# Attention features and a Fourier mixer on one core: rows in blocks of 32, heads in pairs, and a new order of the work

## The chip, the core and the metric

The kernel runs on one core of a Trainium2 chip. A core has TensorE (PE in the profile; its weight loads are PEld), VectorE (DVE), ScalarE (ACT), GpSimd (POOL) and SyncE (SP, which here only issues DMAs). The engines run side by side, each works through its own instructions in order, and semaphores make one wait for another. DMAs are issued by SP, ACT and POOL and run on 16 DMA engines that all three share; those from POOL are queue q0 in the profile, those from SP queue q1. The metric is the time of one execution on the device in microseconds (us), the median of several runs.

## The reference

Inputs: q, k, v of 8 batches x 8 heads x 576 rows x 64, float32; a projection w_phi 64 x 128; two weights of a feed-forward layer, 512 x 2048 and 2048 x 512.

```python
def phi(x):
    proj = np.einsum('bhsd,df->bhsf', x, w_phi)
    proj = proj - np.max(np.abs(proj), axis=-1, keepdims=True)
    return np.concatenate([np.exp(proj), np.exp(-proj)], axis=-1)
q_p, k_p = phi(q), phi(k)
kv = np.einsum('bhsf,bhsd->bhfd', k_p, v);  z = np.sum(k_p, axis=2)
attn = np.einsum('bhsf,bhfd->bhsd', q_p, kv) / (np.einsum('bhsf,bhf->bhs', q_p, z)[..., None] + 1e-06)

x = attn.transpose(0, 2, 1, 3).reshape(B, S, H * D)            # 8 x 576 x 512
u = x + np.real(np.fft.fft(np.fft.fft(x, axis=1), axis=2))
un = (u - mean(u)) / np.sqrt(var(u) + 1e-06)                    # over the last axis
out = u + np.maximum(un @ w_ch1, 0.0) @ w_ch2
```

## The kernel before

One batch (576 rows) is the unit of work, and eight batches follow one another in a pipeline. For each batch k and q are turned so that their 64 features lie on the partitions (KT, QT), multiplied by w_phi on TensorE, and the row maxima of the absolute value are taken by DVE (MK, MQ). ACT forms both exponentials (KPp, KPn, QPHP, QPHN). The factor that the maximum puts on a row is moved elsewhere: for k it multiplies v (VCp, VCn, V4P, V4N, done by POOL), for q it is the ratio E2 of the negative half to the positive half, which DVE multiplies in when the two halves of a head are combined (`tg`, `cb`), before the division (`rd`, and X by POOL). The Fourier transform along the rows uses its symmetry: row r and row 576 - r are folded together (R, CEO), so rows are stored in an order in which a row and its mirror stand on the same partition. The row transform gives DT and ET (from psums `psD` and `px`, with `pm` for the mean row), the column transform gives `pu`, which is added to X. The normalised rows UN are turned to UT (by TensorE in batch 0, by DMA transposes in the others), the first feed-forward product gives `psf` and HT, the second `pso`, and the result is stored.

The 576 rows stand in five chunks of up to 128: chunks 0 and 1 hold rows 1 to 256 (even and odd), chunk 4 holds the 64 rows 0 and 257 to 319, and chunks 2 and 3 hold rows 320 to 575. Before, rows stand in blocks of 16 within the chunks, turned round block by block; q is loaded as it comes (QS01, QS23), the projection reads it through a pattern with a negative step, and the maxima, which stand in load order, are put in order by two matmuls with a 0/1 matrix TURN (`weigh_q`, psum `pt`). TURN itself is built by DVE from counted numbers.

Batch 0 has code of its own. Its float32 inputs are loaded by SP into the space of tiles that are used later: k and q into that of W2b (as KF, Q01, Q23), the last 64 rows and v into that of HT (`load_first`); TensorE turns them (`turn_part`, psum `pst`). SP's loads are issued in the order k, its last 64 rows, k, q 1 to 256, q 320 to 575, the last q rows, the last v rows, v. The weights W1b (2 MB in bfloat16) and W2b are loaded and cast by POOL's DMAs (`load_ffn_weights`), as are k, q and v of the later batches (KS, QS, VS). While batch 0 is prepared, TensorE has little to do, and `stir` runs 60 matmuls on a constant.

What runs when is written out by hand. Each part of the work is a generator (`STREAMS`): F is the feed-forward layer of a batch in 68 steps, M the key-value products, combination and Fourier mixing, T the exponentials, P the maxima of q, R those of k, S the scaling of v, N the normalisation, W the load of the weights, Z the memsets of padding, C and H the constants, G and J the first turns, Y the `stir` matmuls, K, V, Q the loads of the later batches. The string `PLAN` has one letter for each step, and the instructions of all engines are issued in this order; an engine never departs from it.

Of the kernel before, what the change touches and what calls it, by code (L numbers as in the profile page):

```python
# [10 lines left out]
ALU = mybir.AluOpType  # L11
# [12 lines left out]
    "CCZCYYZYGGCTZVTRZKGTGRZWGJTTSJYRSJTQTTPPYTYRPTJMRJTMSMMSPSTKPTPTZMYTMMQTMTPMCQTMMTMTBDMHKMHKHDDHYAHY"  # L24
    "DYMYMHYTMMVMRTQMTNMMYTNTQNNYSFNMFNFNRVRFSTTPTFMFRSYUNTFWMURFVFFFFUUMTPMFBSTFMNTUTPNUSMFVPPCTFMFTUPQM"
    "TFMFTFPATVMFFFMMFTFMFKMFFMQFMFRTKFMFFRFPFDFFFFTFFFFTDFFFDRTFFFMFFTTDMFRFFFFSFFMFFFTFMSMFRFTMTTNMTFMN"
    "FPTMMFSSMTPMFTPPMTFFFMFFQNMPTFBSFMFFQMFFPTFFMNNUAMFFMFMFVTRTFFMFFVRVFFKMFKFFFFTMFMFFFFQMFPFDFFTPFRFF"
    "FTFDPFFTFFDDFFRFFTMFFFTMFFMMBSFFMSFRFTMMTFTNNFMFMMMKFTFMTSTFFFFSMPPTMTFFFFFMFSFMFPTMQQVFFFPTKFFMNNNM"
    "FFMFFMFFUMFFMFMFFFAMTRTVFFRTVFFFFFQMFFFDFDFTFFFDRFTPDFFFTPFFRFFTMFFFFTMMMFSFFRSFTMFTFMTTFNFTFMFNSMMM"
    "FMBSFKTTMQNFFFNPFMTFFFMFTPPFMFSFMNFPQMUTFVFKFPAFFMMFMFFVMFFMTFMFFMFFFMRTFRVFFTFFFQMFFFFTDDFRFFFFTFDP"  # L30
    "FFDFTPFFFRFTMTFFFFFMMMFFRFSFSTMSTFFMTFTFFNMFFTNMMMMSTTFMFFQNFTFPMFFFMFVNFMTBPPFSFMFFTPFMKFFFMFFQPNMF"
    "FMAUKFFMFFFMTTFRFRFMFFFTSFFFFVTMFFFRMTQFFFMTFFFFDFDFFFRFDFTFFDMFTFMFFMFSMFMRFTFFTMFTFTFFTMNNFPSMMMMV"
    "TFFSMTPMSTQFFMTPMFTFBQMFPPPFFMFFMFNVFPFFANNUMFFMFMTFMFFMFFMFFRTFRMFFFFFFFVTTPFSFFRFVFFMTFDFFTFFFDFDR"
# [7 lines left out]
def kernel(  # L41
# [39 lines left out]
    magic = const.tile([128, 1], F32, name="magic")  # L81
    nc.vector.memset(magic[:], -MAGIC)
# [25 lines left out]
    TURN = const.tile([128, 2, 128], F32, name="TURN")  # L108
# [39 lines left out]
    def count_first():  # L148
        count(pc_i[:, 0:1], [[1, 1]], 0, 1)
        count(pc[:, 0:2], [[1, 2]], 225, 2)  # L150
        count(pc[:, 2:3], [[1, 1]], 256, 1)
        nc.gpsimd.memset(pc[0:1, 2:3], 0.0)
        for j in range(2):
            count(
                rs[:, 128 * j:128 * j + 128].rearrange("p (a r) -> p a r", r=16),
                [[-32, 8], [2, 16]], 225 + j, 0,
            )
        count(rs[:, 256:NK], [[1, 64]], 256, 0)
        nc.gpsimd.memset(rs[:, 256:257], 0.0)
        count(tn[:, 0, :], [[1, 128]], 0, -1)  # L160
        nc.vector.tensor_single_scalar(
            out=ident[:], in_=tn[:, 0, :], scalar=0.0, op=ALU.is_equal
        )
        count(pc[:, 3:4], [[1, 1]], 128, -1)
        count(rc.rearrange("p (a r) -> p a r", a=2), [[1, 2], [2, 256]], 0, 0)

    def count_rest():
# [8 lines left out]
        count(tn[:, 1, :], [[1, 128]], 0, 1)  # L176
# [5 lines left out]
    def constants(b):  # L182
        nc.vector.tensor_single_scalar(
            out=pc_i[:, 1:2], in_=pc_i[:, 0:1], scalar=4, op=ALU.arith_shift_right
        )
# [5 lines left out]
        nc.vector.tensor_scalar_mul(out=pn[:, 0:3], in0=pc[:, 0:3], scalar1=1.0 / S)
        nc.vector.tensor_scalar_mul(out=pn[:, 3:4], in0=pc[:, 3:4], scalar1=1.0 / C)
        for j in range(3):
# [29 lines left out]
        yield  # L223
        for t, n in enumerate((112.0, 15.0)):
            nc.vector.tensor_scalar(
                out=blk[:, 1 + t:2 + t], in0=pc_i[:, 1:2], scalar1=64.0 * t - 32.0,
                scalar2=n, op0=ALU.mult, op1=ALU.add,
            )
            nc.vector.tensor_scalar(
                out=TURN[:, t, :], in0=tn[:, t, :], scalar1=blk[:, 1 + t:2 + t], scalar2=None,  # L230
                op0=ALU.is_equal,
            )
# [60 lines left out]
    def make_q(b):  # L293
# [4 lines left out]
            (QS[:], q[b, :, at:at + 256, :].rearrange("h (p j) d -> p h (j d)", j=2))  # L298
            for QS, at in ((QS01, 1), (QS23, 320))
# [23 lines left out]
    def load_first():  # L323
# [105 lines left out]
    def features(b):  # L429
# [977 lines left out]
```

## Time and profile before

| | |
|---|---|
| runs | 426.52 us median of 3 (426.04 to 428.52) |
| profiled execution | span 423.1 us from the first to the last instruction; its runs' median is 3.4 us above the span |
| busy, of the span | PE 94%, PEld 61%, DVE 78%, ACT 72%, POOL 49% |
| chain that ended last | PE 61%, DVE 20%, ACT 8%, POOL 5%, DMA 2%, issue 2% |
| TensorE clock granted | 0.999 of full speed |
| DMA | 42.70 MB, mean 101 GB/s |

Rows of groups read: line, engine, operation, output <- inputs, shapes, count | total busy us, mean ns of one | idle time of the engine just ahead. The mean of a matmul is its length in the pipeline; several overlap, so the total divided by the count is the distance from one to the next. Rows of the timeline read: start us, duration us, engine, line, operation, and in square brackets how long the engine was idle before it and what ended that. Rows of stretches give for each engine its busy us and the number of instructions, then the granted clock, the DMA engines' busy share and GB/s. DMA rows give packets, MB and the share of 16 engines' time.

### The profile page before, as it was taken

What the parts mean: (1) busy time and instruction counts of PE and PEld (TensorE: products, weight loads), DVE (VectorE), ACT (ScalarE), POOL (GpSimd) and SP (SyncE); (2) the same over time, 40 slices, a digit from 0 to 9 for tenths busy, and PEclk for the clock granted to TensorE, in tenths of its full rate; (3) what the DMA queues carried; (4) which work ended last, traced back from release to release, by engine and by line L of the source; (5) the groups of instructions that cost most, each with busy time, mean ns of one, the idle gap of its engine ahead of it and who ended that gap; (6) DMA issues with size and microseconds to landing.
All of it is one profiled execution on the core that took longest, in us unless ns stands there. A gap on an engine that the chain in (4) does not pass through costs nothing.

```text
span 423.1 us, 10390 instructions
## 1 busy us (share of the span) xinstructions
PE 397.4 (94%) x4093; PEld 256.1 (61%) x4122; DVE 331.1 (78%) x681; ACT 306.3 (72%) x626; POOL 207.8 (49%) x271
## 2 busy tenths in 40 slices
PE   8787798999899999999999999999999999999995
PEld 3454475744676558655675558665766567656563
DVE  4989788798979976998779885898989786968103
ACT  6978799748975899489847898588868887353460
POOL 7982688525646077706673282834755331500000
PEclk9999999999999999999999999999999999999999
DMA  8999959984569468853899069954895081103313
GB/s 218 206 165 163 148 88 174 145 83 76 89 102 180 72 101 106 123 84 49 112 153 138 2 91 136 131 71 66 117 138 77 14 102 32 27 0 72 72 26 87
DMA packets 108761, 42.70 MB, mean 101 GB/s; under 512 B 82857, under 2 KB 103721, under 8 KB 108713
## 3 DMA queue, kind: packets, MB, share of 16 engines
q0 software_dynamic: 45936, 16.60, 37.1%
q1 hardware_dynamic: 62215, 24.85, 34.8%
q8 instruction: 32, 0.52, 0.5%
q10 hardware_dynamic: 562, 0.59, 0.5%
q14 instruction: 16, 0.13, 0.1%
HBM read 36.77 MB, written 9.44 MB: 109 GB/s over the span
## 4 chain that ended last, share of the span: by engine, by line
PE 61%; DVE 20%; ACT 8%; POOL 5%; DMA 2%; issue 2%; DVEq 0%; ACTq 0%; POOLq 0%
PE psf L1224 21%; PE pso L1241 19%; DVE R L903 3%; PE kv L887 3%; DVE cb L999 3%; DVE tg L994 2%; PE pso L1267 2%; PE psD L1045 2%; DMA UT<-UN 2%; PE pu L1104 2%; PE psq L547 1%; DVE MK L511 1%; PE psk L491 1%; PE psh L597 1%; DVE X L1094 1%
## 5 line engine op out<-in xcount | busy, mean ns | idle before, releaser
L1224 PE MATMUL psf<-UT,W1b 128*128 128x320 bf16 (+1 forms) x1024 | 142.5, 286 | 2.4 <-DMA UT<-UN 1.5
L1241 PE MATMUL pso<-W2b,HT 128*128 128x512 bf16 x467 | 117.1, 379 | 1.7 <-issue 0.5
L1224 PEld LDWEIGHTS <-W1b 128*128 128x128 bf16 x1024 | 94.0, 98 | 29.7 <-issue 4.3
L1229 ACT ACTIVATE HT<-psf 128x320 bf16<-128x320 f32 x128 | 53.5, 442 | 27.0 <-PE psf L1224 21.6
L1241 PEld LDWEIGHTS <-HT 128*128 128x128 bf16 x496 | 44.8, 98 | 44.6 <-issue 2.6
L1002 POOL TENSOR_TENSOR X<-cb,rd 128x320 f32<-128x320 f32 x56 | 41.5, 746 | 38.6 <-DVE rd L1001 37.3
L466 POOL TENSOR_TENSOR VCn<-VS,VCn 128x512 bf16<-128x512 bf16 x28 | 29.7, 1061 | 38.1 <-ACT VCn L461 35.3
L1231 ACT ACTIVATE HT<-psf 128x512 bf16<-128x512 f32 x64 | 37.9, 605 | 12.6 <-PE psf L1224 12.0
L555 DVE TENSOR_REDUCE MQ<-psq 128x8 f32<-128x1024 f32 (+1 forms) x32 | 34.3, 1084 | 13.4 <-PE psq L547 13.2
L1247 DVE SCALAR_TENSOR_TENSOR X<-pso,rs,X 128x512 f32<-128x512 f32 x31 | 22.8, 735 | 21.6 <-PE pso L1241 21.6
L497 ACT ACTIVATE KPn<-psk 128x1024 bf16<-128x1024 f32 x28 | 28.6, 1021 | 14.0 <-DVE MK L511 13.9
L497 ACT ACTIVATE KPp<-psk 128x1024 bf16<-128x1024 f32 x28 | 28.7, 1025 | 11.1 <-PE psk L491 11.1
L451 POOL TENSOR_TENSOR V4N<-VS,V4N 64x256 bf16<-64x256 bf16 x14 | 8.7, 623 | 53.9 <-ACT V4N L447 53.4
L511 DVE TENSOR_REDUCE MK<-psk 128x8 f32<-128x1024 f32 x28 | 33.9, 1212 | 1.0 <-ACT KPp L497 0.7
L1094 DVE TENSOR_TENSOR X<-pu,X 128x512 f32<-128x512 f32 (+3 forms) x49 | 23.3, 526 | 11.2 <-PE pu L1104 8.9
L466 POOL TENSOR_TENSOR VCp<-VS,VCp 128x512 bf16<-128x512 bf16 x28 | 29.7, 1059 | 0.0
L606 ACT ACTIVATE QPHP<-psh 128x1024 bf16<-128x1024 f32 x28 | 28.9, 1031 | 0.8 <-PE psh L597 0.6
L606 ACT ACTIVATE QPHN<-psh 128x1024 bf16<-128x1024 f32 x28 | 29.0, 1035 | 0.0
L1150 ACT ACTIVATE UN<-X,MV 128x512 bf16<-128x512 f32 (+1 forms) x35 | 24.5, 723 | 5.4 <-DVE MV L1175 3.1
L1174 DVE BATCH_NORM_STATS2 st<-X 128x6 f32<-128x512 f32 (+1 forms) x40 | 27.1, 677 | 0.3
L1190 POOL TENSOR_TENSOR rs<-VE,mhalf 128x5 f32<-128x5 f32 (+1 forms) x9 | 10.3, 1145 | 29.0 <-DVE VE L1189 29.0
L987 PEld LDWEIGHTS <-QPHP 128*128 128x128 bf16 x280 | 21.2, 99 | 4.6 <-DVE cb L999 1.0
(465 smaller groups left out, 825.0 us busy)
## 6 DMA issues: line engine op xcount, KB each, us to landing
out_dram<-X SPq DMA_DIRECT2D x15, 256.0 KB
out_dram<-X SPq DMA_DIRECT2D x60, 64.0 KB
QS<-in_q_dram POOLq DMA_DIRECT2D x14, 256.0 KB, 6.2
KS<-in_k_dram POOLq DMA_DIRECT2D x7, 512.0 KB, 7.4
VS<-in_v_dram POOLq DMA_DIRECT2D x14, 256.0 KB, 5.1
W1b<-in_moe_w_ch_dram POOLq DMA_DIRECT2D x1, 2048.0 KB, 13.1
W2b<-in_moe_w_ch_dram POOLq DMA_DIRECT2D x1, 2048.0 KB, 14.8
W2b<-in_k_dram SPq DMA_DIRECT2D x2, 512.0 KB
```

The source lines that it names most:

```text
L466: nc.gpsimd.tensor_tensor(out=VC[:, hs, :, 0:D], in0=values[b][0][:, hs, :].rearrange("p h (j d) -> p h j d", d=D), in1=VC[:, hs, :, D:D + ...
L497: nc.scalar.activation(out=KP[:, hs, :, :].rearrange("p e (jp jj) f -> p jj (e jp) f", jj=2), in_=psk[:], func=AT.Exp, scale=sgn,)
L511: nc.vector.tensor_reduce(out=MK[:, 2 * pr:2 * pr + 2, :].rearrange("p e (jp jj) -> p jj (e jp)", jj=2), in_=tiles[pr][:], axis=AX.X, op=A ...
L555: nc.vector.tensor_reduce(out=o, in_=i[:], axis=AX.X, op=ALU.max, apply_absolute_value=True)
L606: nc.scalar.activation(out=o, in_=psh[:], func=AT.Exp, scale=sgn)
L1002: nc.gpsimd.tensor_tensor(out=X[:, :, D * h:D * h + D], in0=cb[:, :, 0:D], in1=rd[:].to_broadcast([128, 5, D]), op=ALU.mult,)
L1094: nc.vector.tensor_tensor(out=to, in0=more, in1=to, op=ALU.add)
L1174: nc.vector.bn_stats(out=st[0:M, :], in_=X[0:M, c, 0:C])
L1224: nc.tensor.matmul(ps, lhsT=W1b[:, cc, 128 * hh:128 * hh + 128], rhs=UT[:, cc, lo:hi], start=(cc == 0), stop=(cc == NCC - 1),)
L1229: nc.scalar.activation(out=HT[:, hh, lo:hi], in_=ps, func=AT.Relu, scale=-1.0)
L1231: nc.scalar.activation(out=HT[:, hh - 1:hh + 1, lo:hi], in_=psw[:].rearrange("p (a n) -> p a n", a=2), func=AT.Relu, scale=-1.0,)
L1241: nc.tensor.matmul(po[:], lhsT=HT[:, hh, at:at + 128], rhs=W2b[:, hh, :], start=(hh == 0), stop=(hh == NHH - 1),)
```

## The change

- Rows stand in blocks of 32 instead of 16. Chunks 0 and 1 are loaded block by block, already in order (four DMAs of 32 partitions instead of one of 128, in every later batch); chunks 2 and 3 still need the turn within a block, which for the maxima is now one `stream_shuffle` on DVE. TURN, its construction and its matmuls go, and with them some of the constants' steps. Stores of chunks 0 and 1 are four instead of eight a batch.
- The maxima of the last 64 q rows are formed on 128 partitions, two head pairs at once: 4 matmuls for 8, a DVE reduction of half the length, a POOL copy that brings the upper half down and a POOL memset.
- Two neighbouring heads are divided and scaled in one go (one `rd`, one X for two heads), in the order 0, 1, 6, 7, 4, 5, 2, 3.
- The second product of the last 64 rows: before, even and odd hidden blocks went to the two halves of the PSUM partitions, 512 columns each, and were added one after the other; now each hidden block goes to both, 256 columns each.
- Batch 0: k is loaded by head pair (four DMAs for two), w_phi by one DMA; the row transform takes two single banks and splits its copies otherwise; one pass of the constants moves from ACT to DVE.
- `PLAN` is another string.

```diff
-        for e in range(2):
-            nc.scalar.dma_start(out=wphi_f[64 * e:64 * e + 64, :], in_=w_phi[:, :])
+        nc.scalar.dma_start(out=wphi_f[:], in_=w_phi[:, :].unsqueeze(0).to_broadcast([2, D, DF]))
-        for g in range(2):
-            hs = slice(4 * g, 4 * g + 4)
+        for n, pr in enumerate(PAIRS):
+            hs = slice(2 * pr, 2 * pr + 2)
             put(KF[:, hs, :], k[0, hs, 0:512, :].rearrange("h (p j) d -> p h (j d)", j=4))
...
         def qmax4():
+            whole = pj.tile([128, 2, 4, DF], F32, tag="pj", name="psq4")
+            for s in range(2):
                 for e in range(2):
                     rr = slice(64 * e, 64 * e + 64)
                     nc.tensor.matmul(
-                        ps[e][:, pr, :], lhsT=QT4[rr, pr, :], rhs=wphi2[rr, :],
+                        whole[:, e, s, :],
+                        lhsT=QT4[rr, 2 * s:2 * s + 2, :].rearrange("p x n -> p (x n)"),
+                        rhs=wphi2[rr, :], start=True, stop=True,
...
+            nc.vector.tensor_reduce(
+                out=m[:, 0], in_=whole[:, :, 0:2], axis=AX.X, op=ALU.max, apply_absolute_value=True
+            )
+            nc.gpsimd.tensor_copy(out=m[0:64, 1], in_=m[64:128, 0])
+            nc.gpsimd.memset(m[64:128, 0], 0.0)
...
         def weigh_q(hs):
-            pt = pk.tile([128, n, 4], F32, tag="pk", name="pt")
-            for t in range(2):
-                nc.tensor.matmul(
-                    pt[:, :, 2 * t:2 * t + 2], lhsT=TURN[:, t, :],
-                    rhs=mq[:, hs, 2 * t:2 * t + 2], start=True, stop=True,
-                )
-            nc.scalar.activation(
-                out=E2[:, hs, 4:5], in_=mq[:, hs, 4:5], func=AT.Exp, scale=2.0
-            )
-            nc.scalar.activation(out=E2[:, hs, 0:4], in_=pt[:], func=AT.Exp, scale=2.0)
+            nc.vector.stream_shuffle(
+                out=mq[:, hs, 2:4], in_=mq[:, hs, 2:4], mask=list(range(31, -1, -1))
+            )
+            nc.scalar.activation(out=E2[:, hs, :], in_=mq[:, hs, :], func=AT.Exp, scale=2.0)
...
         for hh in range(NHH):
-            g = 64 * (hh % 2)
-            nc.tensor.matmul(
-                po[g:g + 64, :], lhsT=HT[:, hh, 512:576], rhs=W2b[:, hh, :],
-                start=(hh < 2), stop=(hh >= NHH - 2),
-            )
+            for g in range(2):
+                nc.tensor.matmul(
+                    po[64 * g:64 * g + 64, 0:256], lhsT=HT[:, hh, 512:576],
+                    rhs=W2b[:, hh, 256 * g:256 * g + 256], start=(hh == 0), stop=(hh == NHH - 1),
+                )
...
-        for h in (0, 7, 1, 6, 4, 2, 5, 3):
+        for h in (0, 1, 6, 7, 4, 5, 2, 3):
...
 PLAN = (
-    "CCZCYYZYGGCTZVTRZKGTGRZWGJTTSJYRSJTQTTPPYTYRPTJMRJTMSMMSPSTKPTPTZMYTMMQTMTPMCQTMMTMTBDMHKMHKHDDHYAHY"
+    "YYZCGZGZTTCGGRTWCRZCTJYTSJTRTGPSYTJSRYPTTPJTJMMYZRSSMMPKTPTTPMMTKTMMTQQPMMMQVTBTCMTHHDYMMHDAYYHYKYDT"
```

What the new string does to the engines' own orders is seen best on POOL and ACT, in batch 0. POOL before, from the first products of the constants (gs) to the first scaled values (V4N, V4P, VCn, VCp from v in HT's space); W1b is the load of the first weight, VS and KS are loads of batch 1, HI, V4P, V4N, QPHP and QPHN are memsets:

```order
L197 TENSOR_SCALAR gs<-ga,pn 128x320 x3
L268 MEMSET QPHP 128x8x64
L268 MEMSET QPHN 128x8x64
L212 TENSOR_SCALAR gc<-gc,pn 128x512
L215 TENSOR_SCALAR gc<-gc 128x512
L218 TENSOR_TENSOR ga<-ga,gc 128x512
L271 MEMSET V4P 128x520
L284 DMA VS_249<-in_v_dram 64x4x64 x2
L271 MEMSET V4N 128x520
L284 DMA KS_265<-in_k_dram 64x8x64
L274 MEMSET HI_105 128x512
L274 MEMSET HI_106 128x512
L93 DMA W1b<-in_moe_w_ch_dram 128x4x2048
```

And of the change, the same place and on to the first values:

```order
L242 MEMSET QPHP 128x8x64
L181 TENSOR_SCALAR gs<-ga,pn 128x320 x3
L242 MEMSET QPHN 128x8x64
L245 MEMSET V4P 128x520
L91 DMA W1b<-in_moe_w_ch_dram 128x4x2048
L245 MEMSET V4N 128x520
L196 TENSOR_SCALAR gc<-gc,pn 128x512
L199 TENSOR_SCALAR gc<-gc 128x512
L202 TENSOR_TENSOR ga<-ga,gc 128x512
L818 TENSOR_TENSOR V4N<-HT,V4N 64x4x64 x2
L818 TENSOR_TENSOR V4P<-HT,V4P 64x4x64 x2
L835 TENSOR_TENSOR VCn<-HT,VCn 128x8x64
```

W1b has moved ahead of the long products of the constants; the small loads of batch 1 have left this place, and all loads of batch 1 now stand behind the last VCp, with the two HI memsets between the second and the third pair of VCn and VCp.

ACT before, from the sines (SS, CS, SD, CD) to the row transform's copies (ET); K4p and K4n are the exponentials of the last 64 rows of batch 1's keys:

```order
L238 ACT_TABLE_LOAD
L238 ACTIVATE SS<-gs 128x960
L242 ACTIVATE CS<-ga,halfpi 128x960
L247 ACTIVATE SD<-ga 128x512
L916 CAST HI_105<-R 1x257
L917 CAST HI_105<-R 1x255
L249 ACTIVATE CD<-ga,halfpi 128x512
L482 ACT_TABLE_LOAD
L482 ACTIVATE K4p<-ps_880 128x512
L483 ACTIVATE K4n<-ps_880 128x512
L1053 CAST ET<-psD 128x289
L1054 CAST ET<-psD 128x289
```

And of the change:

```order
L212 ACT_TABLE_LOAD
L212 ACTIVATE SS<-gs 128x960
L216 ACTIVATE CS<-ga,halfpi 128x960
L221 ACTIVATE SD<-ga 128x512
L223 ACTIVATE CD<-ga,halfpi 128x512
L882 CAST HI_103<-R 1x257
L883 CAST HI_103<-R 1x255
L459 ACT_TABLE_LOAD
L459 ACTIVATE K4p<-ps_852 128x512
L460 ACTIVATE K4n<-ps_852 128x512
L474 ACTIVATE KPp<-psk 128x2x4x128
L1024 CAST ET<-psD 128x289
```

One large exponential of batch 1's keys (KPp from psk) now stands ahead of the ET copies; on TensorE the matmuls of ps and of this psk have moved ahead of `pm`, where before ps stood behind `pm` and psk behind the row transform.

More of the change, by code (lines that the diff above doesn't have):

```diff
@@ L29 @@
[L29 to L33, printed above, removed]
@@ L148, in count_first @@
     def count_first():
-        count(pc_i[:, 0:1], [[1, 1]], 0, 1)
-        count(pc[:, 0:2], [[1, 2]], 225, 2)
+        for a in range(4):
+            count(pc[32 * a:32 * a + 32, 0:2], [[1, 2]], 193 - 64 * a, 2)
         count(pc[:, 2:3], [[1, 1]], 256, 1)
@@ L222, in constants @@
         )
[L223 to L232, printed above, removed]
         yield
@@ L518, in qmax4 @@
         def qmax4():
-            if b < 2:
-                ps = [pb.tile([64, 4, DF], F32, tag="pb", name="psq4") for e in range(2)]
-            else:
-                whole = pj.tile([128, 2, 4, DF], F32, tag="pj", name="psq4")
-                ps = [whole[0:64, e] for e in range(2)]
-            for pr in range(4):
+            whole = pj.tile([128, 2, 4, DF], F32, tag="pj", name="psq4")
+            for s in range(2):
                 for e in range(2):
@@ L981, in heads @@
         folds[b] = folded(X, R, HI)
+        held = []
         def combine(h, kvh):
@@ L1319, in fetch_q @@
         staged[b], pieces = make_q(b)
-        for which in ((0,), (1,), (2, 3)):
+        for which in ((0, 1, 2, 3), (4,), (5, 6)):
             load(pieces, which)
```

138 lines of the change are left out of this document (70 added, 68 removed).

## The prediction

> **What bounds the kernel now.** I read the page's busy times, then the same by stretch, then the chain.
>
> ```profile
> PE 397.4 (94%) x4093; PEld 256.1 (61%) x4122; DVE 331.1 (78%) x681; ACT 306.3 (72%) x626; POOL 207.8 (49%) x271
> ...
> 0.00:80.00 80.00, 65.75 (x803) 42.60 (x804) 63.48 (x148) 67.85 (x135) 57.43 (x89) 1.00 1.09 165
> 80.00:380.00 300.00, 293.54 (x3034) 189.29 (x3057) 253.32 (x507) 223.54 (x463) 149.17 (x182) 1.00 0.70 89
> ...
> L1338 PE MATMUL idle<-ones_b 128*128 128x512 bf16 x60 | 17.6, 422 | 1.4 <-DVE keep L130 1.1
> ```
>
> There are two regimes. From 80 to 380 us TensorE (the first number after the length) is busy 293.5 of 300 us; only 6.5 us is idle, so there the time is the amount of matmul work. In the first 80 us it is busy 65.75, and 17.6 us of that is the `stir` filler, so about 32 us does nothing useful. There the chain runs through other engines:
>
> ```profile
> by line: POOL VCn L869 10.0%; POOL VCp L869 9.6%; POOL gc L215 8.5%; PE kv L887 6.4%; issue 5.9%; POOL V4N L852 4.0%; POOL VS L284 4.0%; POOL ga L218 4.0%; POOL V4P L852 3.9%; POOL gs L197 3.7%; PE psn L697 3.5%; POOL HI L274 3.2%; POOL QS
> ...
> 15.71 0.79 POOL L93 DMA_DIRECT2D W1b<-in_moe_w_ch_dram  x1
> 16.51 1.34 POOL L852 TENSOR_TENSOR V4N<-HT,V4N 64x256 bf16<-64x256 f32 x2
> 17.92 1.31 POOL L852 TENSOR_TENSOR V4P<-HT,V4P 64x256 bf16<-64x256 f32 x2
> 19.31 1.06 POOL L869 TENSOR_TENSOR VCn<-HT,VCn 128x512 bf16<-128x512 f32 x1
> 29.82 0.92 POOL L284 DMA_DIRECT2D KS<-in_k_dram  x1
> ```
>
> The first line is the chain between 4 and 36 us. POOL works nearly without pause to the last scaled value tile, which ends where the KS load is issued, near 29.9 us; the last key-value products and the attention of batch 0 follow. So there are two questions: what the new order does to these 30 us, and how much matmul work goes.
>
> **Opening: the load of W1b.** In POOL's new order it stands behind the first constants and three memsets.
>
> ```profile
> 3.47 0.14 DVE L183 TENSOR_SCALAR pc_i<-pc_i 128x1 int32<-128x1 int32 x1
> 4.03 0.17 DVE L191 TENSOR_SCALAR pn<-pc 128x3 f32<-128x3 f32 x1
> 4.39 1.57 POOL L197 TENSOR_SCALAR gs<-ga,pn 128x320 f32<-128x320 f32 x3 [1.23 <-DVE pn L192]
> 6.35 0.53 POOL L268 MEMSET QPHN<- 128x512 bf16 x1
> ```
>
> POOL's first products wait for `pn`; the three small DVE operations before it go (3.47 to 4.03, 0.56 us), so they start at 3.83 and end at 5.40. One memset fits into the wait ahead, two (1.06 us) follow: W1b is issued at about 6.5 us, not 15.71. At that time SP's loads of batch 0 are still on the way; V is only issued from 8.86 us on:
>
> ```profile
> q1 hardware_dynamic: 5793, 3.54, 83.1%
> ...
> 8.86 2.52 SPq L336 DMA_DIRECT2D HT<-in_v_dram  x4
> ...
> 12.66 0.63 PE L368 MATMUL pst<-ident,W2b 128*128 128x128 f32 x4 [0.43 <-DMA W2b<-in_q_dram]
> ```
>
> The first row is the window from 0 to 16 us: 5793 packets, 83.1% of 16 engines, 37 ns each. TensorE already waits for a q tile at 12.66. Now W1b comes in between. How two queues share the engines is seen where they meet (first pair 21 to 27 us, W1b beside the transposed load of KT4; second pair 75 to 78 us):
>
> ```profile
> q0 software_dynamic: 293, 1.20, 98.3%
> q1 hardware_dynamic: 275, 0.07, 8.7%
> ...
> q0 software_dynamic: 863, 0.27, 83.7%
> q1 hardware_dynamic: 846, 0.22, 62.0%
> ```
>
> They take turns packet by packet, 293 to 275 and 863 to 846, however large a packet is. W1b's are 4.1 KB and 322 ns (98.3% of 16 x 6 us over 293); its 2 MB are 512 of them, 32 to an engine, 10.3 us. While it runs, SP's queue sends only 512 of its packets. What comes late in that queue (second q tile, V) therefore lands 10.3 us later, unless plain copies share otherwise than transposes do (a rival). Before, its 13.3 us of work (83.1% of 16) began some 2 us in and ended near 15.4; now they end near 25.7, and usable perhaps 1.5 us later.
>
> What this costs: V's small tile, four products (2.65 us) and eight of 1.04 us have to follow, with two HI memsets (1.06 us by the memset above) now between the pairs. The second pair's V at 27.2 gives 27.2 + 2.1 + 1.0 + 4.2 = 34.5; if POOL's own queue binds (V4 at about 24) it is 36. I take 35.6, **+5.7 us** against 29.9. The other chain agrees: the q tile of 12.66 comes near 22.9, some 10 us late, and DVE's maxima behind it, which kept DVE busy to here,
>
> ```profile
> 31.70 0.29 DVE L740 CAST mt<-pt 96x128 bf16<-96x128 f32 x1 [0.77 <-PE pt L735]
> ...
> 44.59 1.28 ACT L482 ACT_TABLE_LOAD   x1 [2.29 <-PE ps L477]
> 48.99 1.01 ACT L497 ACTIVATE KPp<-psk 128x1024 bf16<-128x1024 f32 x1
> ...
> 41.72 0.38 PE L1021 MATMUL pm<-HI,ones_b 128*128 128x512 bf16 x1 [1.81 <-ACT HI L917]
> ```
>
> end near 37.5 instead of 32.0, since other work has been done by then. The cover of the edits in the constants (one ACT pass less, one DVE pass more), of K by pair and of the one load of wphi is this DMA wait: they count nothing, at most 2 us if it is gone.
>
> Part comes back. ACT waits 2.29 us for `ps` ahead of its table load; the new order puts ps, one psk and their exponentials (K4, KPp, KPn, V4: the two of psk alone are 2.0 us) around that load, work that stood behind it from 46 us on. Worth 0 to 5; I take **-2.5**. The split of the row transform into single banks for batch 0 moves small copies from ACT to DVE, beside each other: 0, within half a us either way.
>
> **Matmul work.** These rows give what goes and comes, on TensorE first:
>
> ```profile
> L563 PE MATMUL pt<-MQ,TURN 128*128 128x16 f32 x28 | 3.6, 243 | 0.0
> L527 PE MATMUL psq<-wphi,QT 64*64 64x128 bf16 x56 | 2.9, 221 | 0.3 <-ACT QPHN L606 0.3
> L1267 PEld LDWEIGHTS <-HT x128: 106/110/110, 104.3 to 414.1; 128*64 128x64 bf16 x128
> L1267 PE MATMUL pso<-W2b,HT 128*64 128x512 bf16 x128 | 16.3, 384 | 0.0
> L1224 PE MATMUL psf<-UT,W1b 128*128 128x256 bf16 x512 | 65.8, 273 | 1.7 <-DMA UT<-UN 1.5
> ...
> L533 DVE TENSOR_REDUCE MQ<-psq 64x8 f32<-64x1024 f32 x6 | 7.3, 1210 | 0.1
> L555 DVE TENSOR_REDUCE MQ<-psq 128x4 f32<-128x512 f32 x8 | 5.1, 683 | 0.9 <-PE psq L547 0.8
> L1001 DVE RECIPROCAL rd<-cb 128x5 f32<-128x5 f32 x56 | 10.7, 191 | 1.9
> L1274 DVE SCALAR_TENSOR_TENSOR X<-pso,rs,X 64x512 f32<-64x512 f32 x16 | 11.9, 744 | 3.9 <-PE pso L1267 3.6
> L1292 DVE SCALAR_TENSOR_TENSOR X<-pso,rs,X 128x256 f32<-128x256 f32 x2 | 1.0, 484 | 1.5 <-PE pso L1286 1.5
> L1002 POOL TENSOR_TENSOR X<-cb,rd 128x320 f32<-128x320 f32 x56 | 41.5, 746 | 38.6 <-DVE rd L1001 37.3
> L284 POOL DMA_DIRECT2D QS<-in_q_dram x28 | 23.2, 830 | 0.2 <-issue 0.2
> DVE tg L994 <- ACT E L570: 3.0, 1, 3.0
> ```
>
> The turning matmuls go: -3.6 us. Half of the last 64 rows' matmuls go: 28 at 52 ns (2.9/56), -1.5. The 64-row output turns 64 pairs of 255 ns (16.3/64) into 128 pairs of half the columns. A pair then lasts what a 256-column matmul lasts, 128 ns (65.8/512): 16.4, **0**. Bounds: -1.5 and, if two weight loads of 110 ns no longer fit under it, +12 us (a rival). Sum **-5.1**, of which some 90% counts, as TensorE is 98% busy there: -4.6.
>
> On DVE 7 x (1.21 - 0.68) + 28 x 0.19 + 16 x (0.74 - 0.48) = 13 us go; the seven shuffles, an operation that the trace does not show, lie between 0.14 (the tiny tensor_scalar above) and 0.68 us each (the small maximum); I take 0.2, near the small rows, +1.4. ACT loses seven small passes. All this lies beside a busier TensorE, so I count none of it except that its 6.5 us of idling may shrink or grow by 2: **-1.0**, since PLAN also puts more forward steps (F) between a batch's second N and its own first F, which reads what N has transposed (fourth batch 5 before, 10 now).
>
> POOL gets more: three further q loads a batch at about 0.83 us each (17 us in all) and 14 small copies and memsets (the shown memset took 0.53); the scaling in pairs takes 28 operations of at most 1.49 us for 56 of 0.746, which is no more. At 149 of 300 us it has room. The new wait: POOL's MQ copy waits for DVE's maxima, behind it stand value products or X, which TensorE and DVE want, and the one exponential E waits for it; DVE waited for E only once, 3.0 us. Halving of the stores frees SP: 0.
>
> **Sum.** The profiled execution has a span of 423.1 us; the median of the runs is 426.5, 3.4 more, which I leave as it is. 426.5 + 5.7 - 2.5 - 4.6 - 1.0 = **424.1 us**.
>
> **Rivals.**
>
> Plain copies do not alternate packet by packet. For it speaks that the rows above show transposed loads only. [...] Then 5.7 falls away: 418.4 us. [...] Chance 0.28.
>
> Slower: the keys of batch 1. TensorE's order now has ps and psk of batch 1 ahead of `pm`, which only waits for HI (its row above: 41.7 before, near 47.4 now). KS is now issued last of all, after 35.6.
>
> ```profile
> 42.04 0.90 POOL L284 DMA_DIRECT2D KS<-in_k_dram  x1 [7.92 <-DMA KT<-KS]
> ```
>
> From issue at 29.82 to the transposed tile took 12.2 us: 36.3 + 12.2 = 48.5, a us late. But seven q and v loads follow directly, and at one for one the transposes may take 4 us more; TensorE then stands at psk till 53, `pm` behind it, and nothing of the 2.5 comes back: 426.5 + 5.7 + 5 - 4.6 = 432.6. It decides from the point at which KT lands after HI. Chance 0.10.
>
> Weight loads of 64 columns do not fit: 424 + 12 = 436, chance 0.04. Against it: in the 256-column row a whole load of 98 ns hides under each matmul. [...]
>
> The forecast itself has 0.55; 0.03 is left for waits in the new order of either sign.
>
> **How the numbers follow.** A per cent (4.3 us) is about what a measurement tells from no change: under 422.2 is faster, above 430.8 slower. The forecast's own uncertainty (shift 3 to 8, return 0 to 5, idling 2) is some 3.5 us, so 0.12 of its 0.55 is faster; with most of the first rival that makes 0.37. Slower: 0.10 + 0.04 less a little, 0.12. Same: 0.51. The range goes from 417 (the first rival less 1.4) to 431 (short of the two slow ones).
>
> **What would show it.** Right: W1b issued near 6.5 us; SP's queue busy past 25 us; TensorE waiting about 10 us for a q tile; last VCp near 35.6; no L563 and a pair of 64-row matmuls every 110 to 130 ns; TensorE idle 4 to 7 us between 80 and 380. Wrong: V landed before 20 us (first rival), psk waiting for KT near 50 us (second), pairs of 220 ns (third), or POOL held for long at the MQ copy.

## The result and the profile after

The changed kernel takes **437.6 us** (median of 4 runs, 436.2 to 440.8) beside 426.3 us for the one before on the same chip: 1.028 times as long, 95% interval 1.022 to 1.033. The forecast was 424.1 us.

The page of the changed kernel (busy times, the granted clock in 40 slices, the chain by engine), and its stretches (length; busy us of PE, PEld, DVE, ACT, POOL; granted clock; DMA share; GB/s):

```profile
PE 399.3 (92%) x4165; PEld 264.1 (61%) x4194; DVE 318.1 (73%) x662; ACT 306.3 (71%) x617; POOL 213.2 (49%) x279
PEclk8959979999989999999999999999999999999998
PE 59%; DMA 18%; DVE 11%; ACT 5%; POOL 4%; issue 2%; SPq 1%; DVEq 0%; POOLq 0%
0.00:80.00 80.00, 65.08 (x704) 40.60 (x705) 57.57 (x133) 61.43 (x117) 56.22 (x93) 0.87 0.87 138
80.00:380.00 300.00, 285.71 (x3106) 191.12 (x3129) 240.92 (x486) 223.54 (x455) 155.80 (x186) 0.99 0.69 96
```

Three things are new. TensorE idles 14.3 of the 300 us in the middle, where it was 6.5. DMAs have 18% of the chain instead of 2%. And the clock, whose mean was 0.999, is down in parts of the first 60 us and near 120 us. About 4.9 us of matmul work went (3.6 for the turn, 0.9 for the last q rows, 0.4 for the 64-row output, by the rows of groups before and after), and still PE's busy time grew by 1.9 us; the stretches at half clock are what the profile shows to set against that.

A table of landmarks, read from the timelines, says where the 11.3 us of span (434.4 less 423.1) came in. First pn is batch 0's first product with the queries, HI the start of the ACT cast that ends the first fold, psf the first matmul of the forward layer of batch 0 and of batch 7. All runs of this study are in it; the experiments are explained below. Each row is one profiled execution, which in e6 was 2.6 us and in e8 5.2 us shorter than the median of the runs, and in e10 4.1, in e11 2.4 and in e12 1.9 us longer.

| kernel | first pn | HI | psf 0 | psf 7 | psf 0 to 7 | span |
|---|---|---|---|---|---|---|
| before | 31.5 | 41.0 | 53.6 | 386.6 | 333.0 | 423.1 |
| changed | 38.9 | 48.4 | 62.3 | 396.9 | 334.6 | 434.4 |
| e1 W1b later | 29.8 | 39.2 | 54.9 | 388.7 | 333.8 | 426.2 |
| e2 before, W1b early | 38.8 | 48.3 | 60.9 | 394.7 | 333.8 | 431.2 |
| e3 new code, old order | 33.2 | 43.0 | 58.2 | 404.0 | 345.8 | 441.0 |
| e4 old code, new order | 37.0 | 46.9 | 61.5 | 408.5 | 347.0 | 445.8 |
| e5 keys early | 35.4 | 44.8 | 57.9 | 391.4 | 333.5 | 429.1 |
| e6 and their load moved | 31.3 | 40.8 | 54.0 | 384.9 | 330.9 | 422.2 |
| e7 e1 with work put back | 29.3 | 38.8 | 54.6 | 390.8 | 336.2 | 428.0 |
| e8 changed, stir in the wait | 38.5 | 48.0 | 61.9 | 395.3 | 333.4 | 432.9 |
| e9 e6, stir ahead of psD | 36.8 | 46.6 | 58.5 | 389.0 | 330.5 | 426.1 |
| e10 e9, stir ahead of psf | 36.9 | 46.6 | 58.5 | 386.6 | 328.1 | 423.7 |
| e11 e10, stir ahead of pt | 35.3 | 44.9 | 56.9 | 384.7 | 327.8 | 421.9 |
| e12 e11, W1b early again | 41.1 | 50.6 | 62.5 | 392.4 | 329.9 | 429.5 |

So against before: +7.4 us to the first pn, +1.3 from there to the first psf, +1.6 over the batches, +1.0 in the tail; forecast were +5.7, -2.5, -5.6 and 0.

The opening of the changed kernel, from the timelines of POOL, TensorE and DVE, with the two DMA queues between 12 and 20 us and two stretches of the clock:

```profile
7.02 0.96 POOL L91 DMA_DIRECT2D W1b<-in_moe_w_ch_dram  x1
q0 software_dynamic: 394, 1.61, 99.2%
q1 hardware_dynamic: 346, 0.09, 8.3%
23.47 0.66 PE L345 MATMUL pst<-ident,HT 64*128 64x64 f32 x4 [4.69 <-DMA HT<-in_q_dram]
25.00:27.50 2.50, 2.38 (x22) 0.95 (x21) 0.97 (x2) 1.00 (x3) 2.27 (x4) 0.50 0.08 25
35.28 1.06 POOL L835 TENSOR_TENSOR VCp<-HT,VCp 128x512 bf16<-128x512 f32 x1
39.09 0.29 DVE L706 CAST mt<-pt 96x128 bf16<-96x128 f32 x1 [0.90 <-PE pt L701]
49.96 0.40 PE L468 MATMUL psk<-wphi,KT 64*128 64x128 bf16 x8 [0.77 <-DMA KT<-KS]
50.29 0.39 PE L994 MATMUL pm<-HI,ones_b 128*128 128x512 bf16 x1
52.23 1.63 PE L1019 MATMUL psD<-SS,CEO 128*128 128x289 bf16 x6 [1.56 <-DVE CEO L1007]
52.50:55.00 2.50, 1.80 (x8) 0.82 (x7) 2.46 (x6) 1.66 (x6) 2.46 (x6) 0.50 0.57 65
```

W1b is issued at 7.02 us. From 12 to 20 us its queue and SP's send 394 and 346 packets. This total alone would also fit turns of several packets each; but in stretches of 0.35 us, the length of one packet of each (322 and 31 ns), both queues send 16 to 18 packets, the same in ten such stretches between 14.6 and 19.4 us. So each of the 16 engines sends SP's plain copies and W1b one for one. TensorE stands 4.69 us before the last q rows, which it uses at 23.47; before, it used them at 14.1 without a wait. The last VCp ends at 36.3, the second `mt`, behind DVE's maxima, at 39.4 (32.0 before), and later psk waits 0.77 us for KT with `pm` behind it, and psD 1.56 us for CEO. Behind the first and the last of these waits the clock is 0.50.

One batch boundary, the fifth batch's, in both kernels (before first): the end of the second normalised tile on ACT and the first psf that reads its transpose.

```profile
247.57 0.72 ACT L1150 ACTIVATE UN<-X,MV 128x512 bf16<-128x512 f32 x1
252.41 1.48 PE L1224 MATMUL psf<-UT,W1b 128*128 128x256 bf16 x12 [0.47 <-DMA UT<-UN]
```

```profile
256.68 0.74 ACT L1133 ACTIVATE UN<-X,MV 128x512 bf16<-128x512 f32 x1
261.62 1.47 PE L1207 MATMUL psf<-UT,W1b 128*128 128x256 bf16 x12 [0.89 <-DMA UT<-UN]
```

From the end of UN to psf it is 4.12 us before (248.29 to 252.41) and 4.20 us after. TensorE waited 0.47 us there; with less to do ahead of it, it waits 0.89. The groups and waits of the changed kernel show the sum of such waits, and the sizes of the edits:

```profile
PE psf L1207 <- DMA UT<-UN: 7.1, 6, 1.7
L1250 PE MATMUL pso<-W2b,HT 128*64 128x256 bf16 x256 | 15.9, 274 | 0.0
L500 PE MATMUL psq<-wphi,QT 64*128 64x128 bf16 x28 | 2.0, 218 | 0.0
L535 DVE STREAM_SHUFFLE MQ<-MQ 128x16 f32<-128x16 f32 x7 | 1.4, 195 | 0.0
```

Six waits of together 7.1 us for UT where there had been two of together 1.5. The 64-row output takes 15.9 us (16.3 before). The matmuls on the last q rows take 2.0 us, 71 ns each, where twice as many took 2.9 us, and the shuffle 0.195 us.

The same from batch to batch, the distance from one first psf to the next in us:

| kernel | 0 | 1 | 2 | 3 | 4 | 5 | 6 |
|---|---|---|---|---|---|---|---|
| before | 58.1 | 46.5 | 47.1 | 47.1 | 48.1 | 45.1 | 41.0 |
| changed | 57.4 | 48.2 | 46.0 | 47.7 | 48.4 | 46.0 | 40.9 |
| e1 | 56.9 | 49.3 | 46.1 | 46.7 | 48.3 | 46.0 | 40.5 |
| e5 | 57.7 | 47.3 | 46.3 | 46.8 | 48.8 | 45.9 | 40.7 |
| e6 | 56.4 | 45.8 | 45.8 | 46.0 | 48.8 | 47.6 | 40.5 |
| e9 | 58.6 | 45.4 | 46.3 | 45.6 | 47.9 | 46.2 | 40.5 |
| e10 | 56.5 | 45.6 | 45.1 | 45.9 | 48.6 | 45.9 | 40.5 |

### The profile page after: what moved, and what is told of

The parts are those of the page before. It is cut to its first block, busy times and chain, and to the rows that moved or that the text cites. A ratio compares the mean times of both kernels' runs of the same rounds, so it can differ in the third digit from the quotient of the medians.

```text
span 434.4 us, 10499 instructions
## 1 busy us (share of the span) xinstructions
PE 399.3 (92%) x4165; PEld 264.1 (61%) x4194; DVE 318.1 (73%) x662; ACT 306.3 (71%) x617; POOL 213.2 (49%) x279
## 4 chain that ended last, share of the span: by engine, by line
PE 59%; DMA 18%; DVE 11%; ACT 5%; POOL 4%; issue 2%; SPq 1%; DVEq 0%; POOLq 0%
PE psf L1207 26%; PE pso L1224 14%; DMA UT<-UN 5%; DMA HT<-in_q_dram 3%; DMA QT<-QS 3%; DMA KT<-KS 3%; PE kv L853 3%; PE psD L1035 2%; DVE cb L969 2%; DVE X L1077 1%; DMA KS<-in_k_dram 1%; DVE tg L962 1%; PE psq L522 1%; PE psk L468 1%; PE pu L1087 1%
## 5 line engine op out<-in xcount | busy, mean ns | idle before, releaser
L1212 ACT ACTIVATE HT<-psf 128x320 bf16<-128x320 f32 x128 | 53.6, 438 | 29.1 <-PE psf L1207 22.9
L1224 PEld LDWEIGHTS <-HT 128*128 128x128 bf16 x496 | 45.4, 98 | 42.8 <-issue 0.7
L975 POOL TENSOR_TENSOR X<-cb,rd 128x640 f32<-128x640 f32 x28 | 35.1, 1255 | 50.1 <-DVE rd L973 44.3
L258 POOL DMA_DIRECT2D QS<-in_q_dram x49 | 33.1, 686 | 2.6 <-DMA QT<-QS 2.6
```

The lines of the kernel that those rows point to most:

```text
L258: nc.gpsimd.dma_start(out=pieces[i][0], in_=pieces[i][1])
L975: nc.gpsimd.tensor_tensor(out=X[:, :, at:at + 2 * D].rearrange("p c (e d) -> p e c d", e=2), in0=cb[:, :, :, 0:D], in1=rd[:].to_broadcast( ...
L1212: nc.scalar.activation(out=HT[:, hh, lo:hi], in_=ps, func=AT.Relu, scale=-1.0)
L1224: nc.tensor.matmul(po[:], lhsT=HT[:, hh, at:at + 128], rhs=W2b[:, hh, :], start=(hh == 0), stop=(hh == NHH - 1),)
```

## The experiments

**The load of W1b, and order against code.** Four runs: W1b later in the changed kernel (e1), earlier in the one before (e2), the new code under the old order (e3), the old code under the new order (e4).

```diff
 e1 (changed kernel)
-YYZCGZGZTTCGGRTWCRZCTJYTSJTRTG
+YYZCGZGZTTCGGRTCRZCTJYTSWJTRTG
 e2 (kernel before)
-CCZCYYZYGGCTZVTRZKGTGRZWGJTTSJ
+CCZCYYZWYGGCTZVTRZKGTGRZGJTTSJ
 e3: the string of before without its last C; e4: the new string with a C behind its last
```

> The changed kernel with one letter moved: the load of W1b is issued after the first scaling step (V4N, V4P) of batch 0 instead of about 7 us. Theory A, W1b in front of the loads of batch 0 costs the opening its 8.7 us (the first psf of batch 0 at 62.3 instead of 53.6): without it V lands near 16, TensorE's wait of 4.69 us for the last q rows and the half clock after it go, the first psf stands near 55 to 57, time 430 to 433 us. Theory B, the rest of the new order or the edits of the code cost the opening: the first psf stays near 61 to 62 and the time above 435 us.

> The kernel before with one letter moved: the load of W1b directly behind the memset of QPHN, about 7 us instead of 15.71. Theory A: W1b's packets take turns with the loads of batch 0 here too, V lands near 25, the first psf comes 6 to 9 us later than 53.6, time 432 to 435 us. Theory B: at most 2 us later, 426 to 428.5 us.

> The changed code under the order of before (its string less the sixth step of the constants, which no longer exists). If the order costs the time and the matmul work that went counts in full: 426.3 - 5 = 421 to 422 us. If the order costs the time, but the saved matmul work is eaten by waits at the start of each batch's forward layer (UT<-UN): 424 to 426 us. If the edits of the code cost the time: 433 us or more.

> The code of before under the new order (with one more letter for the sixth step of its constants). If the order costs the time: 437 to 443 us, the first psf near 62, with waits for UT<-UN. If the edits of the code do: 426 to 429 us.

e1 took 427.9 us (ratio to before 1.004, 1.001 to 1.006), e2 433.7 (1.019, 1.015 to 1.023). One letter is worth 9.7 us in the one kernel and 7.6 us in the other (beside 426.1): theory A holds, and with a larger price than the 5.7 us of the forecast. In e2 the shift stays at 7.3 to 8.1 us to the end, and this wait of TensorE tells why:

```profile
PE kv L887 <- POOL VCp L869: 4.3, 2, 4.1
```

e3 took 443.0 us (1.040, 1.037 to 1.043) and e4 447.4 us (1.052, 1.048 to 1.055). My either-or was wrong: neither the order nor the code alone is the loss, since each order fits its own code better than the other's. In e4 the first psf is 7.9 us late, about what W1b's early place costs, and 14.0 us more lie over the batches. In e3 DVE stands before the folds, because a pair's X comes later than a single head's:

```profile
DVE R L869 <- POOL X L975: 13.7, 7, 4.7
```

It is 3.7 us in the changed kernel. What e3 loses, 12.8 us over the batches, I did not follow further; it only shows that the edits can't be priced under the old order.

**Keys of batch 1, and a load that POOL stands before.** In e1 the opening still lacks its return, and the third batch starts late. Both have a row. TensorE, then POOL, TensorE and the clock around 120 us in e1:

```profile
42.20 0.61 PE L468 MATMUL psk<-wphi,KT 64*128 64x128 bf16 x8 [2.13 <-DMA KT<-KS]
116.67 0.69 POOL L258 DMA_DIRECT2D KS<-in_k_dram  x1 [6.89 <-DVE MQ L530]
117.83 1.06 POOL L443 TENSOR_TENSOR VCn<-VS,VCn 128x512 bf16<-128x512 bf16 x1
119.96 0.29 PE L853 MATMUL kv<-VCp,KPp 128*128 128x65 bf16 x4 [2.15 <-POOL VCp L443]
120.00:130.00 10.00, 9.72 (x115) 7.37 (x116) 5.23 (x13) 7.74 (x13) 5.40 (x7) 0.83 0.90 105
```

The K load of batch 4's last rows stands two steps behind the transposes (B) that empty its buffer; POOL waits for them 6.89 us (the name of the releaser is inferred; the DVE operation ran beside the transpose), with scaled values queued behind.

```diff
 e5: both K letters of batch 1 moved up, to ahead of W1b
-TSWJTRTGPSYTJSRYPTTPJTJMMYZRSSMMPKTPTTPMMTKTMMT
+TSKKWJTRTGPSYTJSRYPTTPJTJMMYZRSSMMPTPTTPMMTTMMT
 e6: e5, and batch 4's first K behind the scaling
-FFFMMBTKMTPMFPTPFMTFFSFMQTP
+FFFMMBTMTPMFPTPFMTFFSFMQKTP
```

> The run with W1b later, and the two loads of batch 1's keys moved ahead of W1b (16 us instead of 28). There psk of batch 1 waited 2.13 us for KT<-KS at 40 us, pm stood behind it on TensorE, and the clock was 0.50 from 42 to 52 us. If the late keys (the prediction's second rival) hold the opening: psk does not wait, the clock stays at 1, the first psf comes 2 to 4 us earlier than 54.9 and the time is 424 to 426 us. If DVE's folding and HI set the end there anyway: first psf at 54 to 55, time 427 to 429 us.

> The same, and the load of batch 4's last 64 key rows (POOL waited 6.89 us at it to 116.7 us, with the MQ copy and the last scaled values of batch 2 behind it) moved behind those. If that wait on POOL's queue is what made TensorE wait 2.15 us for VCp at 117.8 and lose its clock (0.83 from 120 to 130 us): another 2 to 4 us less than the run with the keys early, 421 to 423 us. If the stage is held by UT<-UN in any case: within 1 us of it.

e5 took 431.1 us (1.013, 1.010 to 1.016), worse than e1, e6 426.7 us (1.001, 0.998 to 1.004). The keys did what was expected behind HI: `pm` follows it by 1.1 us in e5 and e6, where e1 had 3.5, and psf by 13.1 and 13.2 us, where e1 had 15.7. But e5's first pn came at 35.4, e6's at 31.3, though both programs are the same to 100 us: there the opening has two courses (last section), so e5's time says nothing on the keys once they have landed. The move itself may have brought the late course: in e1 POOL pauses 1.33 us at 22.5 us, and DVE's small operations on the q maxima, which run in that pause, take 0.16 to 0.18 us; with two K loads ahead POOL scales 1.6 us later, without a pause, and beside it they take up to 1.2 us. The moved load is read from the stage that it stands in, batch 1: 49.3 us in e1 and 47.3 in e5, 45.8 in e6, so **1.5 to 3.5 us**, with the clock up:

```profile
108.93 1.06 POOL L443 TENSOR_TENSOR VCn<-VS,VCn 128x512 bf16<-128x512 bf16 x1
115.58 0.71 POOL L258 DMA_DIRECT2D KS<-in_k_dram  x1 [3.14 <-DMA KT<-KS]
120.00:130.00 10.00, 9.88 (x122) 6.00 (x119) 8.96 (x19) 4.54 (x9) 5.90 (x6) 1.00 1.08 142
```

**What the saved matmul work is worth.** e7 is e1 with that work put back.

```diff
-            for s in range(2):
+            for s in (0, 1, 0, 1):
...
+            pt = pk.tile([128, 8, 4], F32, tag="pk", name="pt")
+            for t in range(2):
+                nc.tensor.matmul(pt[:, :, 2 * t:2 * t + 2], lhsT=ident[:],
+                                 rhs=mq[:, hs, 2 * t:2 * t + 2], start=True, stop=True)
             nc.vector.stream_shuffle(
```

> The run with W1b later, with the matmul work that the change took away put back as repeats without use: 4 more matmuls on the last 64 q rows and the two float32 matmuls of the turn a batch (5.1 us of TensorE in all), results unchanged. If TensorE has no slack, as the prediction had it: 427.9 + 4.6 = 432 to 433 us. If the batches start their forward layer when UT lands, and TensorE waits out what it saved: 428 to 429.5 us.

e7 took 430.9 us, 3.0 more than e1 by the medians: between the two theories. Of the 5.0 us put back (4.3 for `pt`, 0.7 for the q rows) some 3 count. That is a rough size: the ratios to before are 1.001 to 1.006 for e1 and 1.010 to 1.019 for e7, 1.7 to 7.7 us apart, so the times alone do not exclude that all of it counts. That part of it was waited out rests on the waits for UT, of e1 and of e7:

```profile
PE psf L1207 <- DMA UT<-UN: 6.1, 5, 1.6
```

```profile
PE psf L1213 <- DMA UT<-UN: 2.4, 2, 1.7
```

3.7 us of waiting for UT went when the work came back, while the waits for VCp and of the `pt` put back grew by 1.9.

**The clock.** e8 puts stir steps into the changed kernel's wait of 4.69 us.

```diff
-TGPSYTJSRY
+TGPSYTYYYYYJSRY
 and the last five Y of the string go
```

> The changed kernel as it is, with 5 of its 15 stir steps (20 matmuls of 0.21 us at full clock) moved into TensorE's wait of 4.69 us for the last q rows, ahead of the transposes that wait. The clock fell to 0.50 at 21 us and came back at 31.5. If idling dropped it: the clock stays at 1 there, TensorE's work from 23.5 to 31.5 us takes half as long, and 1 to 4 us go, 433.5 to 436.5 us. If the clock has nothing to do with idling, or DVE alone sets the pace after 23.5: 437 to 439 us.

e8 took 439.9 us (1.030, 1.023 to 1.037): nothing gained. The clock did stay up, at 1.00 in both stretches, where the changed kernel's is 0.50:

```profile
22.50:25.00 2.50, 2.38 (x16) 0.95 (x17) 0.00 (x0) 0.94 (x2) 1.11 (x2) 1.00 0.88 251
25.00:27.50 2.50, 1.89 (x28) 1.11 (x28) 2.15 (x4) 1.55 (x4) 2.27 (x4) 1.00 0.11 36
```

but the first pn came only 0.4 us earlier. So idling had dropped the clock, and up to the first pn that cost next to nothing: q, V and the DVE and POOL work on them must set the pace there. The time of e8 says less, since its five steps are missing later: its clock is 0.6 in the slice of its page from 54 to 65 us, where the changed kernel's is 0.7. e9 and e10 do the same elsewhere, on e6: constant matmuls into the psum of psD, where CEO is waited for, and ahead of four first psf.

```diff
 e9, in along_rows of batch 0, behind the tile psD
+                    for x in range(0 if mt else 4 + 2 * i):
+                        nc.tensor.matmul(ps[:], lhsT=ones_b[:], rhs=(ones_b, 512 columns), ...)
 e10 also, in hidden
+                if lo == 0 and hh == 0 and b in (1, 4, 5, 6):
+                    for x in range(6 if b in (1, 5) else 4):
+                        nc.tensor.matmul(psw[:], lhsT=ones_b[:], rhs=(ones_b, 512 columns), ...)
```

> The run with the keys early and their load moved, and 6 and 4 matmuls on a constant written into the psum of the row transform ahead of its two first groups, where TensorE waited 1.56 and 1.25 us for CEO (42.2 and 44.9 us) and ran at a clock of 0.50 from 45 to 51 us. If idling in those two waits dropped the clock, and the slow clock is what ate the return of the exponentials formed earlier: clock 1 there, the first psf at 52 to 53 instead of 54.0, time 423.5 to 425.5 us (against 426.7 with a spread of 423.1 to 428.4). If ACT and DVE set the pace of the row transform: the clock stays up, the first psf at 54, time 426 to 427 us.

> The same, and 4 to 6 such matmuls (0.21 us each) ahead of the first psf of batches 1, 4, 5 and 6, where TensorE waited 1.59, 0.88, 1.69 and 0.90 us for UT<-UN, and after which the clock fell in batch 5 (0.72 from 295 to 300 us). If TensorE has nothing else to do there and its clock is what these waits cost beside their length: 1 to 3 us less than without them, with no half clock in batches 1 and 5. If the waits differ from run to run, so that the matmuls stand in the way as often as they help: within 1 us, or 1 to 2 us more.

In e9 the clock is 0.9 or more in the slices of its page from 43 to 64 us, where e6's was 0.50 from 46 to 50, and from HI to the first psf it is 11.9 us beside 13.2 in e6: here the clock had cost 1.3 us. Its times fell in two groups, 419.9 and 422.7 us and four of 427.6 to 428.4; the ratio of 0.989 (0.985 to 0.993) is of the lower two alone, so e9's time decides nothing. e10 took **421.4 us** (median of seven, 419.3 to 425.9; ratio 0.986, 0.984 to 0.989, without the two highest): less than both kernels, than the one before by 1.1 to 1.4%. The wait for UT that TensorE is left with:

```profile
PE psf L1220 <- DMA UT<-UN: 0.2, 1, 0.2
```

The filler takes the place of the waits. It costs nothing there, but it is not what makes e10 the shorter profile: the batches that it leads take the same in both (45.4 and 45.6, 47.9 and 48.6, 46.2 and 45.9 us in batches 1, 4 and 5). The difference of 2.4 us from psf 0 to 7 lies in batches 0 and 2. In batch 0 it stands already ahead of the first filler of psf (the `ph` before it comes at 113.40 and 111.30 us); what makes that of batch 2 I did not find. In batch 0 of e9 TensorE waited 2.0 us for QT near 86 us and lost its clock (0.50); in e10 it waited 1.2 there and kept it (1.00; e9, then e10):

```profile
90.00:92.00 2.00, 2.00 (x16) 1.07 (x14) 1.93 (x5) 1.19 (x3) 0.17 (x1) 0.50 0.75 107
```

```profile
90.00:92.00 2.00, 2.00 (x11) 0.94 (x10) 1.93 (x5) 0.52 (x2) 0.96 (x1) 1.00 0.50 75
```

Such a fall, with the 0.8 us of longer wait, costs some 2 us (58.6 beside 56.5; batch 5 of e6, 47.6 beside 45.9) and comes in one run and not in the next. The last two runs: e11 adds filler ahead of the first `pt`, e12 is e11 with W1b early again.

```diff
 e11, in turn_m behind the tile pt
+            for x in range(24 if outer else 0):
+                nc.tensor.matmul(pt[:], lhsT=ones_b[:, 0:96], rhs=ones_b[:], start=True, stop=True)
 e12
-YYZCGZGZTTCGGRTCRZCTJYTSKKWJTRT
+YYZCGZGZTTCGGRTWCRZCTJYTSKKJTRT
```

> The run with matmuls on a constant ahead of psD and of four psf, and 24 small ones (128 columns, about 55 ns each) ahead of the first turn of m of batch 0 (pt), where TensorE waited 2.8 us for DVE in the profiles with a late opening (first pn near 36.8, clock 0.50 behind it) and 1.19 us in the one with an early opening (31.3, clock 1). If the length of this wait decides whether the clock falls, and the clock makes the two openings: the clock stays at 1, the first pn at 31 to 33 us in every run, times of 419 to 421.5 us without the group near 425.7. If the two openings come from how DVE's small casts fall beside POOL's scaling: both groups stay, median 420 to 426 us.

> The same with the load of W1b back at its early place (about 7 us) as in the changed kernel. If W1b's cost is the late landing of q and V: 6 to 7.5 us more than without, about 426 to 428 us. If most of the 9.7 us that it cost the changed kernel was the clock after the waits: at most 4 us more, 423 to 425 us.

e11 took 421.3 us (0.987, 0.985 to 0.990), from 418.9 to 425.2: the spread stayed, and in the profile the wait at `pt` was still 1.73 us and the clock 0.50 from 30 to 34 us. The filler was too short to tell, and the other theory, of DVE beside POOL, has the row (last section). e12 took 429.5 us (1.009, 1.006 to 1.012), **8.1 us** more than e11, where most of the cost being the clock would have made it 4 at most. In the profiles the first psf comes 5.6 us later (62.5 for 56.9), and some 2 us lie in batch 0 (58.3 for 56.5), where e12's clock is 0.8 in the slice from 86 to 97 us and e11's 0.9 or more. So most of what W1b's early place costs is the late landing of q and V. In e12's opening the clock was not held, though (0.50 from 22 to 34 us); that this costs little rests on e8 (0.4 us to the first pn).

## Why the prediction was wrong, step by step

| step | forecast | measured |
|---|---|---|
| W1b early, to the first pn | +5.7 | +7.4; on the time 7.6 to 9.7 (e2, e12, e1) |
| exponentials earlier, first pn to psf | -2.5 | +1.3 |
| matmul work | -4.6 | about -3 (e7, a rough size) |
| idling and clock, over the batches | -1.0 | about +4.6 (the +1.6 of the landmarks, plus those 3) |
| tail | 0 | +1.0 |

**The opening's shift** was right in mechanism and place: issue near 6.5 (7.02), one packet for one, last VCp near 35.6 (36.3). The first rival is out, since SP's plain copies take turns of one packet too, 16 to 18 packets of each queue in every 0.35 us. That W1b would cost the opening nothing under that rival (418.4 us) was my estimate, and no run shows it. The step that was undersized is the translation of a late landing into time. POOL's chain came 6.4 us later (36.3 for 29.9). DVE's came 7.4 us later: the second `mt` ended at 39.4, where the prediction had it end near 37.5 instead of 32.0, and the first pn moved by the same 7.4. TensorE used the last q rows 9.4 us later (23.5 for 14.1), and DVE's maxima had to follow; that other work had been done by then saved less than the prediction took off for it. "TensorE waiting about 10 us for a q tile" was off as well: it waited 4.69 us, for the last q rows.

**The return of 2.5 us** did not come. From HI to the first psf it was 12.6 us before and 13.9 in the changed kernel; with the keys early 13.2, with the clock held as well 11.9. So with both mended at most 0.7 us came back, and that it is the exponentials' is not shown, since the edits changed batch 0's row transform too. Late keys (the second rival, with a chance of 0.10 and a price of 5) took 0.7 and a slow clock with its waits 1.3 (e5, e6, e9). That rival happened beside the forecast, not instead of it, and smaller.

**The matmul work** was nearly right in its sum: 4.9 us went for 5.1. The q rows' matmuls saved 0.9 instead of 1.5, since each of the wider ones takes 71 ns and not 52, and the 64-row output saved 0.4 instead of 0. But it was counted at 90%, because TensorE was busy 98% of the middle. Busy is not bound: at the batch boundary shown a chain of 4.2 us runs from UN over two transposes to psf, and TensorE had so far nearly filled it. What is saved ahead of psf can be waited out there, as the waits for UT in e1 and e7 show. e7 prices the real part at about 3 of 5 us, with the spread said above.

**The idling** is the step that failed worst, with its sign: TensorE's idle time from 80 to 380 us rose from 6.5 to 14.3 us, and 7.1 us in all were waits for UT. I argued from the number of forward steps between a batch's second N and its first F, but those steps lie on TensorE, while UT comes over the normalisation and the DMA transposes; that this is why they did not help is argued, not tested. Two more things that the new order did were not in my sum at all: a K load two letters behind the transposes that free its buffer (1.5 to 3.5 us, e6), and a clock that fell to 0.50 behind waits of 1.56, 1.73 and 2.0 us (some 2 us each time in the batches). With the load mended and filler in the waits, the last three profiles take 45.6 us or so in batch 1 where the changed kernel took 48.2, and two of them 327.8 and 328.1 us from psf 0 to 7, 4.9 to 5.2 less than before, near the 5.6 that I had forecast for it: the saving is there, but the order as it was given spent it.

**Right** were the 64-row output (a pair of its matmuls every 124 ns, 15.9 us over 128 pairs; third rival out, though each weight load of 64 columns still lasts 106 to 110 ns in the trace), the shuffle (0.195 us for 0.2) and POOL's new work. Its MQ copy takes 0.19 us; POOL stood 11.5 us in all ahead of the seven copies, which the prediction had named as a sign of being wrong, but no wait of TensorE is put down to them. That fewer stores cost and gain nothing was not tested alone.

**The tail's** 1.0 us: of it 0.6 lie behind the last matmul, which ends 5.4 us ahead of the span's end for 4.8 before. I did not take it apart.

## What to carry to other kernels

A large load moved ahead of others costs what it delays, here one packet of its own for each of theirs and 7.6 to 9.7 us, through everything that waits on the last of them: find the last small piece behind it in the queue. Ahead of a chain of fixed length (normalise, transpose by DMA, first matmul) saved matmul work was worth here only what was not waited out at the chain's end (about 3 of 5 us in e7), however busy TensorE was; measure it by putting the work back. When a wait on TensorE grows, look at the granted clock behind it (here 1.56 us was followed by 6 us at 0.50), and when an order was made for one version of the code, price an edit only together with an order that fits it.

## What was not expected of the hardware

**The clock.** Before, a wait of 1.81 us for HI left it at 1.00 (to 48 us); in the changed kernel 1.56 us (for CEO at 52.2) and 1.73 us (for UT at 119.7) brought it to 0.50, for 6 and 3 us. The wait for QT in batch 0 even went both ways at one length: 1.97 us at 91.4 us left the changed kernel's clock at 1.00, 2.0 us brought e9's to 0.50. So the length of one wait alone does not decide; what else does, no run here shows.

**Two courses of the opening.** DVE has four small operations on `m` (128 x 20). These rows show the last three while POOL scales values, and two of them again afterwards, from e11's timelines of DVE and POOL:

```profile
24.25 1.00 DVE L697 TENSOR_TENSOR ml<-MQ,m 128x20 f32<-128x20 f32 x1
25.28 0.98 DVE L698 CAST m<-ml 128x20 bf16<-128x20 f32 x1
26.29 0.98 DVE L699 TENSOR_TENSOR m<-ml,m 128x20 bf16<-128x20 f32 x1
32.41 0.18 DVE L697 TENSOR_TENSOR ml<-MQ,m 128x20 f32<-128x20 f32 x1
32.63 0.18 DVE L698 CAST m<-ml 128x20 bf16<-128x20 f32 x1
...
24.15 1.06 POOL L839 TENSOR_TENSOR VCn<-HT,VCn 128x512 bf16<-128x512 f32 x1
25.17 1.06 POOL L839 TENSOR_TENSOR VCp<-HT,VCp 128x512 bf16<-128x512 f32 x1
26.18 1.06 POOL L839 TENSOR_TENSOR VCn<-HT,VCn 128x512 bf16<-128x512 f32 x1
```

They take 0.18 us where POOL scales nothing and 1.0 us beside its scaling, and there each ends as POOL's does (25.25 and 25.21, 26.26 and 26.23, 27.27 and 27.24). What makes them end together is not shown. `pt` waits for the last of the four, by 2.8 us in the profiles of e5, e9 and e10, whose clock then fell (0.7 or 0.8 in the slices from 21 to 43 us) and whose first pn came at 35.4 to 36.9, and by 1.2 us in e6's, whose clock held (1.00 from 30 to 42 us). In e6 the last three take 0.99, 0.89 and 0.99 us too; the difference is the first, a cast that takes 0.33 us there and 1.19 in e5. In e1, where POOL pauses, all four take 0.16 to 0.18 us and the first pn comes at 29.8. That this decides between the two groups of times is argued from these profiles, not shown by a run.
